# Scores of three batches on half-height PE tiles, and signs of six weight chunks made by ACT and POOL

## The chip, the cores and the metric

The kernel runs on one core of a Trainium2 chip. Time is device time in microseconds of one execution of the whole program. The core has a matrix engine (PE), which multiplies a stationary operand of up to 128 x 128 (loaded by PEld) with a moving one of up to 512 columns and writes PSUM; a vector engine (DVE); an activation engine (ACT); GpSimd (POOL), which cannot read PSUM; and a queue engine (SP), which here issues every DMA. Each engine works through its own instructions in program order, and waits on semaphores for the others.

## What is computed

Eight batches, eight heads, 512 positions (S), 32 states (NS) and head width 64 (D):

```python
scores = scale * x @ state.T;  a  = softmax(scores)   # over the 32 states
xread  = a @ state                                    # 512 x 64 a head
scores2 = scores.T;            a2 = softmax(scores2)  # over the 512 positions
sread  = a2 @ x                                       # 32 x 64 a head
y = concat([xread, sread], axis=positions)            # 544 rows of 512 channels
gate = sigmoid(causal_conv(y, conv_w, 5 taps))
out  = (gate * (y @ w_val)) @ w_out
```

x and state are float32. w_val, conv_w and w_out arrive as 64-bit floats (512 x 512, 5 x 512, 512 x 512); the kernel turns each into float32 by integer operations on its two 32-bit words.

## The kernel before

**Order by hand.** The program is a list of steps (`op(...)`), numbered as they are defined; ORDER lists these numbers in the order in which they are issued, and a letter behind a number names the engine where a step can run on several (a ACT, v DVE, g POOL). What an engine does next is thus fixed by ORDER alone. Tiles come from rings of a few buffers (`tiles`); a step that takes a buffer anew waits for the readers of what was in it.

**Weights.** For each of the four 128-row chunks of w_val and w_out, `words` issues five steps on 128 x 512 elements: `words_scale` (L205; the upper word read as a float, times 2^-112, into wc), `words_low` (L213; the lower word shifted right, into ws), `words_clamp` (L218), `words_join` (L223; wc shifted left, or ws) and `words_sign` (L228; sign bit of the upper word, or ws). The last runs on DVE and writes the weight: wv for w_val, ws in place for w_out. The words of a chunk lie in buffers shared with other tiles (vw0, ow0 with al; vw1, ow1 with swl), two of each; SP's load of a w_out chunk waits until the steps on the w_val chunk before it in that buffer are done. Each w_out chunk is then split in a high part `woh` (`high`, L234) and a low rest `wol` (`low`, L237), which the final projections use.

**Batches 0 to 2 (LONG)** load x in long runs of memory: partition p holds positions 4p to 4p+3. `x_T` (L303) transposes two positions (a pair, u = 0 or 1) of one head at a time, so that rows 0 to 63 of xT belong to u = 0 and rows 64 to 127 to u = 1. `long_scores` (L333) multiplies xT with the states over all 128 rows; `long_state` holds, for each u, the states in that half and zeros in the other, put there by `long_clear` (six memsets on POOL) and `long_T` (twelve scales). The output is written with stride so that the positions of a head come out in order. Batches 3 to 7 use `scores` (L311), with 64-row tiles, from the start.

**After the scores** a batch goes two ways. Over the states: `scores_T` (L387, 32 x 32 block transposes into sl), `max_n`, `sub_n`, `exp_n`, `sum_n`, `scale_n` and `probs` (L411, transpose back); then, but for batch 0, `high` and `low` split the probabilities into ah and al. Over the positions: `max_s` (L344), `exp_s` (L347, with a sum read out), `exp_T` (PE transposes), `state_read`. `read` (L416) makes xread in four PSUM tiles xr, which share the ring of the scores (sc, four buffers). `gate_first`, `gate_tap`, `gate_last`, `gate_add`, `gate` make the gate from xr. For batch 0 the convolution is done by PE (`read_conv`, L430) and `gate_read` (L451, ACT) makes the gate straight from PSUM. `values` (L475) multiplies the probabilities with state times w_val; `gated` (L486) joins both, `high` and `low` split g into gh and gl, and `project` (L496) multiplies with w_out: twelve matmuls per 128 positions, which need gh and gl of all four chunks of the batch. `project_copy` and `store` end it. The 32 state rows of all batches are done at the end (`tail`). `warm_up` (L240) is PE work without use, placed by ORDER.

Of the kernel before, what the change touches and what calls it, by code (L numbers as in the profile page):

```python
# [9 lines left out]
F32 = mybir.dt.float32  # L10
# [12 lines left out]
P = 128  # L23
# [46 lines left out]
def state_attention_gated_kernel(  # L70
# [45 lines left out]
        nb=(4, [P, NG], F32), sum2=(4, [P, NG], F32), r2=(2, [P, NG], F32),  # L116
# [5 lines left out]
        wc=("g", F32), ws=("o", I32), sTl=("last", F32), z5=("zc", F32), vw0=("al", I32), vw1=("swl", I32), ow0=("al", I32), ow1=("swl", I32),  # L122
# [23 lines left out]
    for name, shape, dt in (  # L146
        ("ident", [P, P], F32), ("wv", [P, NPR, C], F32), ("woh", [P, NPR, C], F32R), ("wol", [P, NPR, C], F32R),
        ("cw", [P, TAPS, NPR], F32), ("ones", [P, 2], F32),
        ("sel", [TAPS * NPR, TAPS, P], F32), ("cwb", [P, TAPS, P], F32),
        ("z", [P, B, NG, D], F32), ("xt", [P, NPR, B, HALO + NS], F32),  # L150
    ):
        fixed[name,] = const.tile(shape, dt, name=name)
    ident, wv, woh, wol, cw, ones, sel, cwb, z, xt = (
        fixed[n,] for n in ("ident", "wv", "woh", "wol", "cw", "ones", "sel", "cwb", "z", "xt"))
# [73 lines left out]
    def words_sign(word, dst, *key):  # L228
        hi = word()[..., 1]
        p, n = hi.shape  # L230
        nc.vector.scalar_tensor_tensor(
            dst().bitcast(I32), hi, SIGN, get("ws", *key)[:p, :n], op0=ALU.bitwise_and, op1=ALU.bitwise_or)

# [87 lines left out]
    def long_clear(b, u):  # L321
        nc.gpsimd.memset(long_state(b, u)[halves(u)[1]], 0.0)

    def long_state(b, u):
        return get("sTl", b)[:, u * H * NS:(u + 1) * H * NS].rearrange("p (k u n) -> p k u n", u=2, n=NS)

    def long_T(e, b, u, t):
        own, to = halves(u)[0], halves(t)[0]
        scale(
            e, long_state(b, t)[to, :, u], get("sgp", 0)[own].rearrange("p (k i n) -> p k i n", k=NPR, i=SB)[:, :, b],  # L330
            SCALE)

    def long_scores(b, g):  # L333
        for u in range(2):
            for q in range(SB):
                h = NG * q + g
                nc.tensor.matmul(
                    get("sc", b, g)[NS * q:NS * q + NS].rearrange("n (p v u) -> n u v p", v=2, u=2)[:, u],
                    long_state(b, u)[:, h // 2, h % 2],
                    get("xT", b, h // 2)[:, h % 2 * 256:h % 2 * 256 + 256].rearrange("d (v p) -> d v p", v=2),  # L340
                    start=True, stop=True, tile_position=(0, NS * q))
# [9 lines left out]

    def exp_T(b, g):
        for j in range(NJ):
            t = get("e2", b, g).rearrange("q (p j) -> q j p" if b in LONG else "q (j p) -> q j p", j=NJ)
            nc.tensor.transpose(get("e2p", b, g)[:, j * P:(j + 1) * P], t[:, j], ident)  # L355
# [14 lines left out]
    def sum_s(b):  # L370
        r2 = get("r2", b)
        nc.vector.tensor_scalar_add(r2, get("sum2", b), EPS)
        nc.vector.reciprocal(r2, r2)
# [195 lines left out]
    def words(src, fn, *key):  # L569
# [4 lines left out]
        op(words_sign, src, fn, *key)  # L574
# [7 lines left out]
    def group(r):  # L582
        op(group_T, r)
        op(state_T, r)
        for b in LONG if r == 0 else ():
            for u in range(2):
                op(long_clear, b, u)
                for t in range(2):
                    op(long_T, b, u, t)
    def batch(b):  # L590
# [10 lines left out]
        if b not in LONG:  # L601
            op(scores, b)
        for g in range(NG):
            if b in LONG:
                op(long_scores, b, g)
            op(scores_T, b, g)
            op(max_s, b, g)
            op(exp_s, b, g)
# [5 lines left out]
        op(probs, b)  # L614
# [120 lines left out]
```

## Time and profile before

| | us |
|---|---|
| three runs | 249.08, 247.27, 248.54 |
| median | 248.54 |
| the profiled execution: time | 247.3 |
| its span on the core | 245.5 |
| ORDER: steps on PE, DVE, ACT, POOL, SP | 188, 289, 268, 93, 85 |

A profile line names source line, engine, operation, and output<-inputs by the program's names. Busy times of the engines overlap; what sets the time is the chain of waits, and the stage in which an engine is full. A row of the stages has, behind the stretch and its length, busy time and count for each engine, the granted clock, the DMA share and GB/s. The trace shows a clock of 1.00 throughout. A matmul of 32-bit floats stands as two or more records.

### The profile page before, as it was taken

How to read it: one execution, taken by the hardware profiler on the slowest of the kernel's cores; microseconds unless marked ns; L12 is line 12 of the kernel's file. 1: busy time of each engine (PE TensorE's matmuls, PEld its weight loads, DVE VectorE, ACT ScalarE, POOL GpSimd, SP SyncE). 2: the span in 40 equal slices, each digit the busy share in tenths (PEclk: the TensorE clock that was granted, in tenths of full speed). 3: DMA queues.
4: the chain of work that ended last, by engine and by line, in shares of the span. 5: the costliest groups of instructions: out<-in, count | busy, mean ns of one | idle time of the engine just before them, and what ended most of it. 6: DMA issues, size and time to landing. Idle time of an engine off the chain costs nothing.

```text
span 245.5 us, 5051 instructions
## 1 busy us (share of the span) xinstructions
PE 231.2 (94%) x1955; PEld 167.7 (68%) x1955; DVE 206.3 (84%) x325; ACT 151.0 (62%) x321; POOL 127.0 (52%) x101
## 2 busy tenths in 40 slices
PE   7976999899999999999999999999999999978994
PEld 7953463366677884866787778666766768867882
DVE  3299999999898998899899898998997899987200
ACT  2056977788647875754787769785696475433110
POOL 3001146289959267793575689928758380131200
PEclk9999999999999999999999999999999999999999
DMA  6939987000320309213801021110110302300224
GB/s 194 312 105 341 340 190 169 7 3 0 88 78 10 85 24 277 62 28 88 225 34 53 3 96 62 69 43 3 43 44 3 132 0 85 128 0 3 85 76 138
DMA packets 34549, 22.88 MB, mean 93 GB/s; under 512 B 26058, under 2 KB 29150, under 8 KB 34526
## 3 DMA queue, kind: packets, MB, share of 16 engines
q1 hardware_dynamic: 34526, 22.57, 30.2%
q8 instruction: 15, 0.25, 0.4%
q14 instruction: 8, 0.07, 0.1%
HBM read 13.65 MB, written 8.91 MB: 92 GB/s over the span
## 4 chain that ended last, share of the span: by engine, by line
PE 62%; DVE 24%; DMA 5%; issue 4%; ACT 2%; SPq 1%; DVEq 0%; ACTq 0%
PE val L484 12%; PE op L492 11%; PE op L494 10%; PE op L493 10%; DMA vw<-w_val 4%; PE xTp L309 3%; DVE acc L461 3%; PE xr L421 3%; DVE tacc L518 3%; PE srp L365 3%; DVE g L487 2%; PE e2p L355 2%; PE sgv L287 2%; PE sc L315 2%; DMA ow<-w_out 2%
## 5 line engine op out<-in xcount | busy, mean ns | idle before, releaser
L461 DVE SCALAR_TENSOR_TENSOR acc<-xr,cw,acc 128x509 f32<-128x509 f32 (+2 forms) x84 | 60.6, 739 | 3.8 <-ACT xt L457 2.7
L492 PE MATMUL op<-woh,gh 128*128 128x512 f32 x128 | 52.1, 407 | 1.5 <-DVE g L487 1.1
L494 PE MATMUL op<-woh,gl 128*128 128x512 f32 x128 | 50.4, 394 | 0.0
L493 PE MATMUL op<-wol,gh 128*128 128x512 f32 x128 | 50.1, 392 | 0.0
L175 POOL TENSOR_TENSOR acc<-acc,last 128x508 f32<-128x508 f32 x22 | 28.6, 1304 | 27.6 <-DVE acc L461 22.5
L175 POOL TENSOR_TENSOR gl<-g,gh 128x512 fp32r<-128x512 f32 x25 | 33.0, 1326 | 9.0 <-ACT gh L162 8.4
L492 PEld LDWEIGHTS op<-woh,gh 128*128 128x128 f32 x128 | 24.0, 188 | 13.5 <-DVE g L487 4.0
L162 ACT COPY o<-op 128x512 f32<-128x512 f32 x26 | 15.3, 590 | 21.6 <-PE op L494 21.6
L175 POOL TENSOR_TENSOR ex<-ex,rc 128x1024 f32<-128x1024 f32 x8 | 15.4, 1919 | 25.3 <-DVE rc L406 23.5
L494 PEld LDWEIGHTS op<-woh,gl 128*128 128x128 f32 x128 | 24.0, 188 | 5.4
L493 PEld LDWEIGHTS op<-wol,gh 128*128 128x128 f32 x128 | 24.1, 188 | 4.6
L484 PE MATMUL val<-ah,swh 128*128 128x512 f32 x56 | 24.1, 430 | 1.1 <-DVE g L487 1.1
L473 ACT ACTIVATE sig<-acc 128x512 f32<-128x512 f32 x28 | 17.8, 637 | 9.1 <-POOL acc L175 6.2
L487 DVE SCALAR_TENSOR_TENSOR g<-sig,val 128x512 f32<-128x512 f32 x32 | 21.5, 674 | 2.2 <-PE val L484 1.0
L309 PE MATMUL xTp<-ident,x 128*128 128x128 f32 x128 | 19.2, 279 | 3.7 <-DMA x<-x 2.2
L162 ACT COPY xT<-xTp 128x512 f32<-128x512 f32 x29 | 17.1, 594 | 9.0 <-PE xTp L309 8.8
L484 PE MATMUL val<-ah,swl 128*128 128x512 f32 x56 | 22.1, 395 | 0.0
L484 PE MATMUL val<-al,swh 128*128 128x512 f32 x56 | 22.1, 394 | 0.0
L456 ACT ACTIVATE acc<-xr,cw 128x512 f32<-128x512 f32 x28 | 19.3, 699 | 4.3 <-PE xr L421 3.9
L162 ACT CAST gh<-g 128x512 fp32r<-128x512 f32 x24 | 15.1, 633 | 9.8 <-DVE g L487 9.8
L309 PEld LDWEIGHTS xTp<-ident,x 128*128 128x128 f32 x128 | 14.3, 140 | 9.9 <-issue 1.9
L175 POOL TENSOR_TENSOR al<-sl,ah 128x1024 fp32r<-128x1024 f32 x7 | 17.1, 2443 | 4.5 <-ACT xt L162 3.6
(132 smaller groups left out, 456.3 us busy)
## 6 DMA issues: line engine op xcount, KB each, us to landing
x<-x SPq DMA_DIRECT2D x32, 256.0 KB
out<-o SPq DMA_DIRECT2D x32, 256.0 KB
vw<-w_val SPq DMA_DIRECT2D x4, 512.0 KB
ow<-w_out SPq DMA_DIRECT2D x4, 512.0 KB
sg<-state SPq DMA_DIRECT2D x8, 64.0 KB
z<-state SPq DMA_DIRECT2D x16, 32.0 KB
out<-to SPq DMA_DIRECT2D x8, 64.0 KB
cww<-conv_w SPq DMA_DIRECT2D x1, 20.0 KB
```

Of the source, the lines that this page charges most:

```text
L162: nc.scalar.copy(out, in_)
L175: (nc.vector if e == "DVE" else nc.gpsimd).tensor_tensor(out, a, b, op=how)
L309: nc.tensor.transpose(get("xTp", b, pr)[:, j * P:(j + 1) * P], t, ident)
L365: nc.tensor.matmul(get("srp", b)[NS * q:NS * q + NS, g * D:(g + 1) * D], get("e2T", b, g)[:, j, NS * q:NS * q + NS], heads[:, j, NG * q + ...
L456: nc.scalar.mul(get("acc", b, pr), pt, cw[:, HALO, pr:pr + 1])
L461: nc.vector.scalar_tensor_tensor(acc[:, d:], get("xr", b, pr)[:, :S - d], cw[:, HALO - d, pr:pr + 1], acc[:, d:], op0=ALU.mult, op1=ALU.add)
L473: nc.scalar.activation(get("sig", b, pr), get("acc", b, pr), AF.Tanh, scale=0.5)
L484: nc.tensor.matmul(get("val", b, k), w, a, start=(i == 0), stop=(i == len(parts) - 1))
L487: nc.vector.scalar_tensor_tensor(get("g", b, k), get("sig", b, k), 1.0, get("val", b, k), op0=ALU.add, op1=ALU.mult)
L492: nc.tensor.matmul(pt, gh, woh[:, k], start=(k == 0), stop=False)
L493: nc.tensor.matmul(pt, gh, wol[:, k], start=False, stop=False)
L494: nc.tensor.matmul(pt, gl, woh[:, k], start=False, stop=(k == NPR - 1))
```

## The change

Two things are changed by hand, and ORDER is written anew for all steps.

**Scores of batches 0 to 2.** The states lie once in a fixed tile `both` (rows 0 to 63 and 64 to 127 hold the same), filled by four `long_T` of 64 x 384 instead of twelve of 64 x 128; the memsets are gone. `long_scores` works on tiles of 64 rows x 32 columns, and writes u = 0 and u = 1 to two PSUM tiles: sc(b, u) has half the positions of all heads, where sc(b, g) had all positions of half the heads. What follows is adapted: `long_max` and `long_max_both` for the maximum over both halves, four `long_exp` of 256 columns for two `exp_s` of 512, sums from two parts, and `long_probs`, which transposes 128 x 256 four times and writes every second element, for one transpose of 128 x 1024.

**Signs.** For chunks 1 and 3 of w_val and all four of w_out, `words_sign` is replaced by two steps: ACT takes the sign of the upper word (as -1, 0 or 1, into a buffer of `sig`), and POOL multiplies it into the joined words.

```diff
-        wc=("g", F32), ws=("o", I32), sTl=("last", F32), z5=("zc", F32), ...
+        sgn=("sig", F32), wc=("g", F32), ws=("o", I32), z5=("zc", F32), ...
+    def words_sgn(word, *key):
+        nc.scalar.activation(get("sgn", *key), word()[..., 1].bitcast(F32), AF.Sign)
+    def words_signed(word, dst, *key):
+        nc.gpsimd.tensor_tensor(dst().bitcast(F32), get("ws", *key).bitcast(F32), get("sgn", *key), op=ALU.mult)
...
-    def long_scores(b, g):
-        for u in range(2):
+    def long_scores(b):
+        for g in range(NG):
             for q in range(SB):
-                h = NG * q + g
-                nc.tensor.matmul(
-                    get("sc", b, g)[NS * q:NS * q + NS].rearrange("n (p v u) -> n u v p", v=2, u=2)[:, u],
-                    long_state(b, u)[:, h // 2, h % 2],
-                    get("xT", b, h // 2)[:, h % 2 * 256:h % 2 * 256 + 256].rearrange("d (v p) -> d v p", v=2),
-                    start=True, stop=True, tile_position=(0, NS * q))
+                for u in range(2):
+                    r = slice(D * u, D * u + D)
+                    c = slice(g * S // 2, (g + 1) * S // 2)
+                    nc.tensor.matmul(
+                        get("sc", b, u)[NS * q:NS * q + NS, c].rearrange("n (p v) -> n v p", v=2),
+                        both[r, q, g, b], get("xT", b, q)[r, c].rearrange("d (v p) -> d v p", v=2),
+                        start=True, stop=True, tile_position=(D * u, NS * q))
...
+    def long_max(b, u):
+        nc.vector.tensor_reduce(
+            get("nbl", b)[:, u], get("sc", b, u).rearrange("p (g t) -> p g t", g=NG), axis=AX.X, op=ALU.max,
+            negate=True)
+    def long_max_both(b):
+        nc.vector.tensor_tensor(get("nb", b), get("nbl", b)[:, 0], get("nbl", b)[:, 1], op=ALU.min)
+    def long_exp(b, g, u):
+        c = slice(g * S // 2, (g + 1) * S // 2)
+        nc.scalar.activation(
+            get("e2", b, g)[:, u * S // 2:(u + 1) * S // 2], get("sc", b, u)[:, c], AF.Exp,
+            bias=get("nb", b)[:, g:g + 1], accum_out=get("suml", b)[:, u, g:g + 1])
...
+    def long_probs(b, u):
+        a = get("sl" if b > 0 else "a0", b).rearrange("p g (t u) -> p u g t", u=2)[:, u]
+        ex = get("ex", b).rearrange("p (u g k) n -> p u g (k n)", u=2, g=NG)[:, u]
+        for g in range(NG):
+            nc.vector.transpose(a[:, g], ex[:, g])
...
-        op(words_sign, src, fn, *key)
+        if key in SIGNED:
+            op(words_sgn, src, *key)
+            op(words_signed, src, fn, *key)
+        else:
+            op(words_sign, src, fn, *key)
```

The new ORDER has 937 steps for 923. On the whole, by engine: PE 198 (warm_up 31 for 18), DVE 298 (low 17 for 10, high 11 for 7), ACT 270, POOL 86 (low 32 for 39, high 7 for 9, sub_n 7 for 5), SP 85. What stands ahead of the first `read` (batch 1), which both orders put after the work of batch 0, and on ACT ahead of the last `gate_read`, before -> after; a kind that isn't named has the same count:

| engine | steps ahead |
|---|---|
| DVE | words_sign 7 -> 2; words_scale 5 -> 2, that of conv_w 1 -> 0; words_clamp 5 -> 6; words_join 7, words_low 8 in both; max_s 6 -> 0, long_max 0 -> 6, long_max_both 0 -> 3; probs 2 -> 0, long_probs 0 -> 4 (of two transposes each); long_T 0 -> 2; sub_n 2 -> 1, scale_n 0 -> 1; copy of xT 1 -> 0; gated 1 -> 0; state_val_low 1 -> 2; read_last_copy 0 -> 1 |
| ACT | words_sgn 0 -> 5; words_scale 3 -> 5; exp_s 4 -> 0, long_exp 0 -> 12; long_T 12 -> 2; state_val_high 2 -> 4; high 13 -> 14; read_last_copy 0 -> 2 |
| POOL | words_signed 0 -> 5 |
| PE | warm_up 15 -> 29; exp_T 3 -> 5; values of batch 0 3 -> 2; read_last 2 -> 3; long_scores of three batches in both |

Behind that read, until the first `project`, DVE has in the new order: one words_join, four gated of batch 0 and one of batch 1, six gate_tap and one gate_add of batch 1, low of the probabilities of batch 1 and four more low, the last of which is gl of the last chunk of batch 0. PE has: that read, state_read of batch 1, the other two values of batch 0, one exp_T, three x_T, two values of batch 1, state_read_T, state_val of batch 3.

SP's order begins before with chunk 3 of w_val, conv_w, two heads of x of batch 0, chunks 1, 0 and 2, the states of batches 0 to 3, the rest of x of batch 0, and chunk 2 of w_out; after with chunks 2 and 3 of w_val, conv_w, chunk 0, two heads of x, the states, the rest of x of batch 0, chunk 1, six heads of x of batch 1, and chunk 3 of w_out.

More of the change, by code (lines that the diff above doesn't have):

```diff
@@ L121, in state_attention_gated_kernel @@
     alias = dict(
-        wc=("g", F32), ws=("o", I32), sTl=("last", F32), z5=("zc", F32), vw0=("al", I32), vw1=("swl", I32), ow0=("al", I32), ow1=("swl", I32),
+        sgn=("sig", F32), wc=("g", F32), ws=("o", I32), z5=("zc", F32), vw0=("al", I32), vw1=("swl", I32), ow0=("al", I32), ow1=("swl", I32),
         sg=("acc", F32), a0=("ah", F32), sw0=("swh", F32),
@@ L148, in state_attention_gated_kernel @@
         ("cw", [P, TAPS, NPR], F32), ("ones", [P, 2], F32),
-        ("sel", [TAPS * NPR, TAPS, P], F32), ("cwb", [P, TAPS, P], F32),
+        ("both", [P, NPR, 2, len(LONG), NS], F32), ("sel", [TAPS * NPR, TAPS, P], F32), ("cwb", [P, TAPS, P], F32),
         ("z", [P, B, NG, D], F32), ("xt", [P, NPR, B, HALO + NS], F32),
@@ L152, in state_attention_gated_kernel @@
         fixed[name,] = const.tile(shape, dt, name=name)
-    ident, wv, woh, wol, cw, ones, sel, cwb, z, xt = (
-        fixed[n,] for n in ("ident", "wv", "woh", "wol", "cw", "ones", "sel", "cwb", "z", "xt"))
+    ident, wv, woh, wol, cw, ones, both, sel, cwb, z, xt = (
+        fixed[n,] for n in ("ident", "wv", "woh", "wol", "cw", "ones", "both", "sel", "cwb", "z", "xt"))
     def two(t):
@@ L317, in scores, with long_T @@
                     start=True, stop=True, tile_position=(D * g, NS * q))
[L321 to L327, printed above, removed]
+    def long_T(e, u, t):
         own, to = halves(u)[0], halves(t)[0]
         scale(
-            e, long_state(b, t)[to, :, u], get("sgp", 0)[own].rearrange("p (k i n) -> p k i n", k=NPR, i=SB)[:, :, b],
+            e, both[to, :, u], get("sgp", 0)[own].rearrange("p (k i n) -> p k i n", k=NPR, i=SB)[:, :, :len(LONG)],
             SCALE)
-    def long_scores(b, g):
-        for u in range(2):
+    def long_scores(b):
+        for g in range(NG):
             for q in range(SB):
-                h = NG * q + g
-                nc.tensor.matmul(
-                    get("sc", b, g)[NS * q:NS * q + NS].rearrange("n (p v u) -> n u v p", v=2, u=2)[:, u],
-                    long_state(b, u)[:, h // 2, h % 2],
-                    get("xT", b, h // 2)[:, h % 2 * 256:h % 2 * 256 + 256].rearrange("d (v p) -> d v p", v=2),
-                    start=True, stop=True, tile_position=(0, NS * q))
+                for u in range(2):
[5 more added lines that the diff above has]
+                        start=True, stop=True, tile_position=(D * u, NS * q))
     def max_s(b, g):
@@ L350, in exp_s @@
             accum_out=get("sum2", b)[:, g:g + 1])
+    def long_max(b, u):
[9 more added lines that the diff above has]
+            bias=get("nb", b)[:, g:g + 1], accum_out=get("suml", b)[:, u, g:g + 1])
     def exp_T(b, g):
         for j in range(NJ):
-            t = get("e2", b, g).rearrange("q (p j) -> q j p" if b in LONG else "q (j p) -> q j p", j=NJ)
-            nc.tensor.transpose(get("e2p", b, g)[:, j * P:(j + 1) * P], t[:, j], ident)
+            if b in LONG:
+                t = get("e2", b, g)[:, j % 2 * S // 2:(j % 2 + 1) * S // 2].rearrange("q (p v) -> q v p", v=2)[:, j // 2]
+            else:
+                t = get("e2", b, g)[:, j * P:(j + 1) * P]
+            nc.tensor.transpose(get("e2p", b, g)[:, j * P:(j + 1) * P], t, ident)
     def exp_T_copy(e, b, g):
@@ L584, in group @@
         op(state_T, r)
[L585 to L589, printed above, removed]
+        for u in range(2 if r == 0 else 0):
+            for t in range(2):
+                op(long_T, u, t)
     def batch(b):
@@ L600, in batch @@
             op(high, lambda pr=pr: get("xT", b, pr), lambda pr=pr: get("xTp", b, pr))
-        if b not in LONG:
-            op(scores, b)
[L603 to L608, printed above, removed]
+        if b in LONG:
+            op(long_scores, b)
+            for u in range(2):
+                op(scores_T, b, u)
+                op(long_max, b, u)
+            op(long_max_both, b)
+            for g in range(NG):
+                for u in range(2):
+                    op(long_exp, b, g, u)
+        else:
+            op(scores, b)
+            for g in range(NG):
+                op(scores_T, b, g)
+                op(max_s, b, g)
+                op(exp_s, b, g)
         op(max_n, b)
@@ L613, in batch @@
         op(scale_n, b)
-        op(probs, b)
+        if b in LONG:
+            for u in range(2):
+                op(long_probs, b, u)
+        else:
+            op(probs, b)
         if b > 0:
```

78 lines of the change are left out of this document (42 added, 36 removed).

## The prediction

> **What bounds the kernel now.** I read the page first, then the stages, then the order of events where one limit hands over to another.
>
> ```profile
> span 245.5 us, 5051 instructions
> PE 231.2 (94%) x1955; PEld 167.7 (68%) x1955; DVE 206.3 (84%) x325; ACT 151.0 (62%) x321; POOL 127.0 (52%) x101
> PE 62%; DVE 24%; DMA 5%; issue 4%; ACT 2%; SPq 1%; DVEq 0%; ACTq 0%
> ```
>
> The chain that ended last is PE for 62% and DVE for 24%. The stages show which of them holds where (columns: stretch, its length, then busy time and count of PE, PEld, DVE, ACT, POOL, then clock and DMA):
>
> ```profile
> 12.00:20.00 8.00, 6.55 (x59) 4.00 (x59) 7.42 (x16) 4.42 (x12) 0.00 (x0) 1.00 0.49 158
> 20.00:30.00 10.00, 7.64 (x78) 4.50 (x79) 9.73 (x17) 8.37 (x19) 1.62 (x4) 1.00 1.03 343
> 30.00:40.00 10.00, 9.54 (x164) 5.66 (x163) 9.90 (x17) 8.49 (x18) 4.89 (x4) 1.00 0.79 182
> 40.00:50.00 10.00, 9.18 (x88) 3.92 (x87) 9.97 (x17) 7.00 (x17) 5.42 (x4) 1.00 0.26 60
> 50.00:95.00 45.00, 44.30 (x389) 31.50 (x388) 42.87 (x66) 32.87 (x71) 32.44 (x23) 1.00 0.21 57
> 95.00:195.00 100.00, 99.99 (x912) 72.29 (x911) 91.23 (x137) 71.51 (x153) 69.90 (x49) 1.00 0.23 70
> 195.00:227.00 32.00, 28.96 (x143) 23.71 (x142) 29.16 (x46) 14.36 (x30) 9.58 (x7) 1.00 0.11 41
> ```
>
> From 12 to 50 us DVE works 37.0 of 38 us and PE has gaps. From 50 on PE is full (44.3 of 45, then 99.99 of 100) and DVE has slack (8.8 us in 95 to 195). So the kernel has a DVE-bound front and a PE-bound rest, and the hand-over is the instruction where PE stops waiting for DVE. That is the read of batch 1:
>
> ```profile
> 47.89 1.47 PE L421 MATMUL xr<-sl,z 32*64 32x512 f32 x16 [0.82 <-DVE sl L412]
> 46.41 1.22 DVE L412 STREAM_TRANSPOSE sl<-ex 128x1024 f32<-128x1024 f32 x1
> 40.17 1.92 POOL L175 TENSOR_TENSOR ex<-ex,rc 128x1024 f32<-128x1024 f32 x1 [0.57 <-DVE rc L406]
> 40.22 2.41 DVE L231 SCALAR_TENSOR_TENSOR ws_o<-ow,ws_o 128x512 int32<-128x512 int32 x1
> 41.07 0.61 ACT L452 ACTIVATE sig<-xr 128x512 f32<-128x512 f32 x1
> ```
>
> PE's read of batch 1 starts at 47.89 and was released by DVE's transpose of that batch's probabilities (L412). Ahead of it, a sign step (L231) that began 0.05 us after a POOL product took 2.41 us, and ended 0.54 us after that product.
>
> So the sum is: how much earlier does read of batch 1 start, and does PE have more or less to do and to wait for behind it. The rows that price the steps (line, engine, shapes, count, busy and mean ns):
>
> ```profile
> L231 DVE SCALAR_TENSOR_TENSOR wv<-vw,ws_v 128x512 int32<-128x512 int32 x4 | 2.7, 683 | 0.0
> L231 DVE SCALAR_TENSOR_TENSOR ws_o<-ow,ws_o 128x512 int32<-128x512 int32 x4 | 5.5, 1375 | 0.0
> L172 DVE TENSOR_SCALAR wc_v<-vw 128x512 f32<-128x512 f32 x4 | 1.7, 424 | 8.6 <-DMA vw<-w_val 8.6
> L221 DVE TENSOR_SCALAR wc_v<-wc_v 128x512 f32<-128x512 f32 x4 | 1.6, 412 | 0.0
> L388 DVE STREAM_TRANSPOSE sl<-sc 128x512 f32<-128x512 f32 x16 | 10.8, 696 | 0.1
> L412 DVE STREAM_TRANSPOSE sl<-ex 128x1024 f32<-128x1024 f32 x7 | 8.6, 1226 | 0.0
> L373 DVE RECIPROCAL r<-r 128x2 f32<-128x2 f32 x8 | 1.3, 166 | 0.3
> L164 DVE COPY xT<-xTp 128x512 f32<-128x512 f32 x3 | 2.0, 660 | 0.0
> L170 ACT ACTIVATE sTl<-sgp 64x128 f32<-64x128 f32 x12 | 3.3, 272 | 12.6 <-PE sgp L276 11.8 <-PE sc L337 0.6
> L170 ACT ACTIVATE wc_o<-ow 128x512 f32<-128x512 f32 x3 | 2.1, 696 | 0.0
> L348 ACT ACTIVATE e<-sc,nb 128x512 f32<-128x512 f32 x16 | 11.0, 689 | 2.7 <-DVE nb L345 2.7
> L348 ACT ACTIVATION_READ_ACCUMULATOR e<-sc,nb 128x1 f32 x16 | 3.2, 202 | 0.0
> L400 ACT ACTIVATE ex<-sl 128x1024 f32<-128x1024 f32 x8 | 8.5, 1062 | 4.0 <-DVE sl L175 2.3 <-POOL sl L175 1.7
> L166 POOL TENSOR_TENSOR gh<-g,ones 128x512 fp32r<-128x512 f32 x6 | 6.3, 1042 | 2.4 <-DVE g L487 2.4
> L175 POOL TENSOR_TENSOR gl<-g,gh 128x512 fp32r<-128x512 f32 x25 | 33.0, 1326 | 9.0 <-ACT gh L162 8.4 <-PE sc L315 0.5
> L337 PE MATMUL sc<-xT,sTl 128*32 128x256 f32 x96 | 6.6, 384 | 0.1
> L315 PE MATMUL sc<-xT,sT 64*32 64x512 f32 x80 | 5.4, 601 | 0.0
> ```
>
> Back to back, an instruction costs some 0.08 us less than its length. In the chain of waits a sign step (0.683 long) stands so:
>
> ```profile
> 15.64 0.61 DVE wv L231
> ```
>
> So I use mean less 0.08 on DVE.
>
> **DVE ahead of the read of batch 1, by the two orders.** Counts are those of the table of the change; only differences count.
> - Signs: five words_sign fewer (7 to 2), 5 x 0.60 = -3.0. One of them was the held one: 2.41 - 0.68 = -1.73 more.
> - words_scale: three fewer on DVE, 3 x 0.34, and the small one of conv_w: -1.15. One clamp more: +0.34.
> - One xT copy fewer (to ACT): -0.6. One sub_n fewer, one scale_n of the same 128x1024 more: 0. One gated fewer, one state_val_low more, both 128x512: 0.
> - long_max has the form of max_s (128x512 in, two results for one): 0. long_max_both is new and tiny; the nearest row is the 128x2 reciprocal, 0.17, so 3 x 0.17 = +0.5.
> - long_T: two of four on DVE, 64x384 out of PSUM, not in the trace. Between 0.27 (ACT, 64x128) and 0.66 (DVE, 128x512); I take 0.5, nearer to the larger: +1.0.
> - long_probs: four 128x256 transposes for one of 128x1024. From 0.696 at 512 and 1.226 at 1024 columns, 0.43 at 256, so 4 x 0.35 = 1.4 against 1.15: +0.3 a batch, two batches, +0.6. Writing every second element shows nowhere; if it halved the rate, each would take 0.70 and a batch +1.3, the upper end; no reason for a gain.
> - One tiny copy: +0.15.
>
> Sum -3.9 us, between -5 and -2. The start I leave at zero: SP issues the same loads first (w_val, conv_w, the states of the first group, x of batch 0), in another order. Read of batch 1 then starts at about 44.0.
>
> **PE.** The three batches' scores fall from 96 matmul records of 128 rows to 96 of 64 rows, two row halves in two banks. The nearest row is L315, where two row halves also alternate, 5.4 us for 5 batches, 1.1 a batch; L337 cost 2.2 a batch. So 1.1 to 2.2 a batch, I take 1.1. The 3.3 us saved lie before 44 us, where PE has gaps, so they count nothing unless PE becomes late there. Likewise the 14 warm-ups more ahead of this read (29 for 15): they lie in PE's gaps (4.3 us of 12 to 40, and the time before the loads land). If that cover goes, they cost 0.45 each, 6.3 at most:
>
> ```profile
> 101.41 0.45 PE warm L243 x4
> 162.04 0.44 PE e2p L355 x4
> 43.37 3.70 PE L484 MATMUL val<-a,sw 128*128 128x512 f32 x8
> ```
>
> Behind the read, PE has one values of batch 0 more to do (3.70 for two: +1.85), two exp_T fewer (-0.88), one warm-up fewer (-0.45), one read_last fewer (-0.15): +0.4. The first project is then released by gl of the last chunk of batch 0. DVE has about 12.0 us ahead of that behind the probabilities (four gated and one of batch 1 at 0.6, six taps at 0.66, a gate_add at 0.9, four low at 0.6, one at 1.15, one join), PE about 11.5 in the same stretch. With the handing over, PE waits about 1.0 us there: +1.0.
>
> **POOL, ACT and SP.** POOL gets six products (1.04 to 1.33 each) and loses six memsets and seven low; it works 1.6 and 4.9 of 10 us in 20 to 40, so I cost them at nothing as POOL time. ACT gets five signs ahead of the read, like words_scale on ACT 0.70 each; its idle time hides them, see the second rival. SP's first w_out load waited for DVE's sign of a w_val chunk; now it waits for ACT's sign of chunk 3, early in ACT's order:
>
> ```profile
> SPq L199 <- DVE wv L231: 3.9, 1, 3.9
> ```
>
> Behind it x of batch 1 was queued, but DVE was busy all along (9.73 of 10 in 20 to 30), so an earlier x frees nothing: 0.
>
> **Sum.** -3.9 + 0.4 + 1.0 = -2.5 us. The profiled execution took 247.3; so 244.8 by it. The median of the three runs is 248.5, 1.2 above that execution; I take half of that: 245.4.
>
> **Rivals.**
> 1. The hold moves instead of going (about 248.6). The ws_o sign steps took 5.5 us for four where 2.7 is normal. Ahead of the read POOL now runs five products of signs, while seven joins stay on DVE with two SBUF inputs, as the sign had. If each product holds a DVE step for half its 1.3 us, 3.2 us come back, and the gain is gone. Against it, no join was held:
>
> ```profile
> L226 DVE SCALAR_TENSOR_TENSOR ws_o<-wc_o,ws_o x4: 670/678/683, 24.6 to 48.1; 128x512 int32<-128x512 int32 x4
> ```
>
> They are 0.683 at most, though POOL was busy a third of 20 to 40. The Trainium skill (SBUF — State Buffer, Who interferes with whom) says that a DVE instruction with two SBUF inputs contends with a GpSimd instruction that reads SBUF, and that the loser blocks for the whole instruction. The 2.41 us agree; by that rule the joins are as exposed as the signs were.
> 2. Slower: ACT becomes the front's limit (about 251.2). Ahead of the last gate_read of batch 0, ACT gets 5 signs (+3.5), 2 words_scale (+1.4), 12 half exponentials for 4 whole ones (a half is 0.689 less 256 columns at 0.373/512, so 0.50, plus 0.20 read-out: 8.4 - 3.6 = +4.8), 5 copies and scales (+2.1), 10 small scales fewer (-2.7): +9.1 us. Before, that gate_read ended at 41.68 (41.07 + 0.61), so 2.3 us remain to 44.0, and ACT's idle time from 12 to 40 is 6.7 us (28 less 4.42, 8.37, 8.49). 9.0 of cover for 9.1: just enough. If ACT fills none of the 6.7, the gate_reads end at 50.8, the read, which needs their PSUM, comes 2.9 later than before, and with the +0.4 the sum is 250.6 by the profiled execution, 251.2 by the same half step as above. There is no gain left once ACT fills less than some 3.3 us of its gaps.
> 3. Sign isn't in ACT's loaded table. One load ran, for exp and tanh together:
>
> ```profile
> L170 ACT ACT_TABLE_LOAD x1 | 1.3, 1283 | 0.7 <-PEq L724 0.7
> ```
>
> Then each sign between exponentials costs two loads, 2.6 us; with three such ahead of the read ACT is 7.7 us later and the time about 255. The Trainium skill (ScalarE: Activation LUTs, Table sets: the hidden batching unit) says that cheap functions stand in every set, naming relu, copy, identity and abs, not sign; it gives some 2.66 us for a switch. No run here shows it yet.
> 4. More than forecast (about 242): DVE also gets the scores of batch 0 earlier, 1.1 us for both halves instead of
>
> ```profile
> 17.28 2.67 PE L337 MATMUL sc<-xT,sTl 128*32 128x256 f32 x32
> ```
>
> and the second held sign, behind the read, goes too (5.5 - 2.7 - 1.73 = 1.1).
>
> **How the numbers follow.** Forecast 0.46, rival 1 0.18, rival 2 0.17, rival 3 0.03, rival 4 0.16. The predicted time is that of the forecast, 245.4. Range 241.8 to 251.2: from rival 4 to rival 2. A measurement of this kernel tells about 1%, 2.5 us, from no change. Faster by more than that is below 246.0: rival 4 and most of the forecast, 0.55. Within: the rest of it, rival 1 and part of rival 2, 0.29. Slower, above 251.0: part of rival 2, rival 3, 0.16.
>
> **What would show it.** Read of batch 1 (PE, xr<-sl,z, its first record) near 44 instead of 47.9, released by DVE. No words_sign held; joins at 0.68. Sign on ACT near 0.7 and a single table load. long_probs pieces near 0.43, long_scores near 1.1 a batch. PE full from about 55 on, DVE some 90% there. I am wrong if that read waits for ACT, if joins or low on DVE show 1.5 us and more beside POOL, if PE gets gaps in 95 to 195, or if DVE comes late for the last gated.

## The result: 2.7% slower, and the profile after

The changed kernel takes 254.59 us (median of 6 runs, 253.75 to 255.11) where the kernel before takes 248.58 in the same measurement: ratio 1.0274, 95% interval 1.0237 to 1.0311. The prediction, 245.4 us within 241.8 to 251.2, was wrong, in sign and in range. The profiled execution took 254.3 us.

Ahead of any row, the account that the rest goes by. TensorE (PE) ends the kernel, so the time is: when the read of batch 1 starts, plus PE's own work behind it, plus what PE waits behind it. For the waits I took every PE step behind that read and counted what it took beyond its shortest instance in the traces of before and after. All numbers in us:

| | read of batch 1 | PE waits behind it | last PE step ends |
|---|---|---|---|
| before | 47.89 | 18.0 | 241.88 |
| after | 47.42 | 25.2 | 248.80 |

The work left over is 176.0 in the one (241.88 - 47.89 - 18.0) and 176.2 in the other; counted by the shortest instances, it tells only that PE's list of steps behind the read weighs nearly the same. So the front gained 0.5 us where I forecast 3.9, and the part behind it lost 7.2 where I forecast 1.0.

The page of the changed kernel: span and size, busy time by engine, and the chain that ended last, which is followed back only a short way here:

```profile
span 252.4 us, 5171 instructions
PE 237.5 (94%) x2007; PEld 173.3 (69%) x2007; DVE 214.2 (85%) x340; ACT 154.2 (61%) x329; POOL 126.7 (50%) x94
PE 6%; DVE 2%; issue 1%; ACT 1%; ACTq 0%
```

DVE is busy for 7.9 us more than before (214.2 against 206.3), though signs were taken from it. The stages of the changed kernel, in the same columns as before:

```profile
12.00:20.00 8.00, 7.94 (x84) 6.44 (x83) 5.28 (x11) 4.08 (x9) 3.75 (x3) 1.00 0.73 261
20.00:30.00 10.00, 9.26 (x112) 6.65 (x100) 9.72 (x18) 9.21 (x23) 1.76 (x2) 1.00 0.78 267
30.00:40.00 10.00, 9.29 (x145) 4.91 (x145) 9.39 (x21) 9.31 (x31) 8.11 (x6) 1.00 0.69 157
40.00:50.00 10.00, 8.71 (x175) 4.92 (x170) 9.73 (x19) 7.53 (x16) 4.91 (x3) 1.00 0.01 2
50.00:95.00 45.00, 44.32 (x326) 29.75 (x325) 43.24 (x71) 32.42 (x68) 24.04 (x16) 1.00 0.38 96
95.00:195.00 100.00, 97.53 (x806) 70.78 (x805) 94.23 (x137) 69.72 (x146) 64.50 (x44) 1.00 0.18 57
195.00:227.00 32.00, 30.53 (x221) 24.23 (x220) 28.91 (x43) 17.30 (x37) 16.41 (x11) 1.00 0.17 63
```

Two rows stand out. In 12 to 20 DVE, the limit of the front, works 5.28 of 8 us where it worked 7.42: it waits there. In 95 to 195 PE has gaps where it had none (97.53 of 100 for 99.99), and DVE works 3.0 us more.

**The front.** In time order on PE, then on DVE (the second number is the length; in brackets the idle time before and what ended it):

```profile
12.51 2.82 PE L251 MATMUL warm<-ident 128*128 128x128 f32 x20
15.16 0.60 PE L284 MATMUL sgp<-ident,sg 128*128 128x128 f32 x4
...
47.42 1.21 PE L451 MATMUL xr<-sl,z 32*64 32x512 f32 x16 [0.59 <-DVE sl L439]
```

```profile
15.96 0.18 DVE L258 COPY cw<-cwp 128x20 f32<-128x20 f32 x1 [2.62 <-PE cwp L255]
...
43.68 2.29 DVE L177 TENSOR_TENSOR ex<-ex,rc 128x1024 f32<-128x1024 f32 x1
...
47.42 1.47 DVE L228 SCALAR_TENSOR_TENSOR ws_o<-wc_o,ws_o 128x512 int32<-128x512 int32 x1
...
148.32 2.40 DVE L429 TENSOR_SCALAR sm<-sm 128x32 f32<-128x32 f32 x1
...
158.28 4.11 DVE L177 TENSOR_TENSOR gl<-g,gh 128x512 fp32r<-128x512 f32 x2
```

Five warm-ups (21 to 25: 20 records, 2.82 us) stand in PE's order ahead of `group_T`, the transposes of the states. DVE has nothing to do until PE has made cwp behind them, and idles 2.62 us.

**The middle.** PE's waits there, and beside them what POOL does at the places where the DVE rows above are long:

```profile
151.71 0.50 PE L514 MATMUL val<-ah,swh 128*128 128x512 f32 x1 [0.61 <-DVE g L517]
...
155.71 0.53 PE L514 MATMUL val<-ah,swh 128*128 128x512 f32 x1 [0.54 <-DVE g L517]
...
162.44 0.51 PE L524 MATMUL op<-woh,gl 128*128 128x512 f32 x1 [0.55 <-DVE gl L177]
...
170.20 1.10 PE L451 MATMUL xr<-sl,z 32*64 32x512 f32 x10 [0.37 <-DVE acc L491]
```

```profile
148.27 2.42 POOL L177 TENSOR_TENSOR al<-sl,ah 128x1024 fp32r<-128x1024 f32 x1
...
158.19 1.32 POOL L177 TENSOR_TENSOR acc<-acc,last 128x508 f32<-128x508 f32 x1 [1.71 <-DVE acc L491]
159.46 2.37 POOL L177 TENSOR_TENSOR ex<-ex,rc 128x1024 f32<-128x1024 f32 x1
```

Each of these PE waits is for DVE. A small add of 128x32 takes 2.40 us, from 0.05 after the start of POOL's low half (al) to its end; the same form takes 0.18 at six other places of this kernel, and 0.92 at one, beside POOL again. Two low halves (gl) take 4.11 together, where one alone takes 0.65 to 0.69. In the count of the table above, PE waits 7.2 us in the steps that start between 148 and 177, 5.2 more than before in the same stretch; before, no step from 93 to 177 waited more than 0.24. The groups say why DVE is there at all (first row before, the others after):

```profile
L175 DVE TENSOR_TENSOR gl<-g,gh 128x512 fp32r<-128x512 f32 x7 | 5.7, 829 | 0.8 <-ACT gh L162 0.7
```

```profile
L177 POOL TENSOR_TENSOR gl<-g,gh 128x512 fp32r<-128x512 f32 x20 | 26.7, 1338 | 17.8 <-ACT gh L164 11.7 <-DVE gh L166 5.7
L177 DVE TENSOR_TENSOR gl<-g,gh 128x512 fp32r<-128x512 f32 x12 | 13.8, 1154 | 0.3
...
L240 POOL TENSOR_TENSOR ws_o<-ws_o,sgn_o 128x512 f32<-128x512 f32 x4 | 5.4, 1352 | 8.9 <-ACT sgn_o L237 7.6 <-DVE nb L361 1.4
...
L439 DVE STREAM_TRANSPOSE sl<-ex 128x256 f32<-128x256 f32 x8 | 2.9, 414 | 0.4 <-POOL ex L177 0.3
L237 ACT ACTIVATE sgn_o<-ow 128x512 f32<-128x512 f32 x4 | 2.8, 708 | 0.0
...
L164 ACT ACT_TABLE_LOAD x1 | 1.3, 1283 | 0.7 <-PEq L767 0.7
```

Five of the 25 low halves that POOL made went to DVE, 5.7 -> 13.8 us: that is as much as DVE's whole increase. At 0.68 us each, the five are an estimated 3.4 us; the other 4.7 are time that low halves spend held beside POOL (their mean goes from 829 to 1154 ns).

**The tail.** ACT's copy of project(7,2) stands behind a gate that waits 4.27 us for DVE, and PE's next project waits for the buffer which that copy frees:

```profile
232.63 0.63 ACT L553 ACTIVATE tsig<-tacc 128x512 f32<-128x512 f32 x1 [4.27 <-DVE tacc L548]
233.17 0.57 ACT L164 COPY o<-op 128x512 f32<-128x512 f32 x1
```

```profile
233.79 0.51 PE L522 MATMUL op<-woh,gh 128*128 128x512 f32 x1 [1.57 <-ACT o L164]
```

### The profile page after: what moved, and what is told of

The parts are those of the page before. It is cut to its first block, busy times and chain, and to the rows that moved or that the text cites. A ratio compares the mean times of both kernels' runs of the same rounds, so it can differ in the third digit from the quotient of the medians.

```text
span 252.4 us, 5171 instructions
## 1 busy us (share of the span) xinstructions
PE 237.5 (94%) x2007; PEld 173.3 (69%) x2007; DVE 214.2 (85%) x340; ACT 154.2 (61%) x329; POOL 126.7 (50%) x94
## 5 line engine op out<-in xcount | busy, mean ns | idle before, releaser
L491 DVE SCALAR_TENSOR_TENSOR acc<-xr,cw,acc 128x510 f32<-128x510 f32 (+2 forms) x84 | 60.0, 739 | 1.6 <-ACT xt L487 0.5
L177 POOL TENSOR_TENSOR acc<-acc,last 128x508 f32<-128x508 f32 x22 | 29.2, 1330 | 23.4 <-DVE acc L491 18.4
L177 POOL TENSOR_TENSOR gl<-g,gh 128x512 fp32r<-128x512 f32 x20 | 26.7, 1338 | 17.8 <-ACT gh L164 11.7
L164 ACT COPY o<-op 128x512 f32<-128x512 f32 x29 | 17.1, 589 | 29.9 <-PE op L524 29.8
L164 ACT COPY xT<-xTp 128x512 f32<-128x512 f32 x31 | 18.3, 607 | 16.7 <-PE xTp L317 16.7
L177 POOL TENSOR_TENSOR ex<-ex,rc 128x1024 f32<-128x1024 f32 x7 | 14.1, 2018 | 21.2 <-ACT o L164 6.4
L503 ACT ACTIVATE sig<-acc 128x512 f32<-128x512 f32 x28 | 17.7, 634 | 10.0 <-POOL acc L177 8.2
L317 PE MATMUL xTp<-ident,x 128*128 128x128 f32 x128 | 18.9, 277 | 1.1 <-ACT xT L164 0.7
L251 PE MATMUL warm<-ident 128*128 128x128 f32 x124 | 17.5, 299 | 1.4 <-POOL ident masks.py:199 1.4
L251 PEld LDWEIGHTS warm<-ident 128*128 128x128 f32 x124 | 16.3, 212 | 1.9 <-POOL ident masks.py:199 1.4
```

The lines of the kernel that those rows point to most:

```text
L164: nc.scalar.copy(out, in_)
L177: (nc.vector if e == "DVE" else nc.gpsimd).tensor_tensor(out, a, b, op=how)
L251: nc.tensor.matmul(get("warm", i)[:, j * P:(j + 1) * P], ident, ident, start=True, stop=True)
L317: nc.tensor.transpose(get("xTp", b, pr)[:, j * P:(j + 1) * P], t, ident)
L491: nc.vector.scalar_tensor_tensor(acc[:, d:], get("xr", b, pr)[:, :S - d], cw[:, HALO - d, pr:pr + 1], acc[:, d:], op0=ALU.mult, op1=ALU.add)
L503: nc.scalar.activation(get("sig", b, pr), get("acc", b, pr), AF.Tanh, scale=0.5)
```

## The experiments

**Theory A**: neither edit of the code costs the time; the newly written order does, at three places: warm-ups ahead of `group_T`, DVE in the middle, the copy in the tail. **Rival B**: the edits themselves collide. **Rival C**: the middle has too much DVE work in any order. **Rival D**: what is saved at one place waits at the next. ORDER's numbers are written below as the steps they stand for, with the letter of the engine behind them; `low<gated(4,1)` is the low half of what gated(4,1) made. Lines left out are marked `...`. Ratios are to the kernel before on the same chip.

**e1: signs alone, e2: scores alone, on the order of before.**

```diff
+words_sgn(o,0)
 words_join(o,0)
...
-words_sign(o,0)
+words_signed(o,0)
```

> The old order and the old scores; only the signs of the six chunks are made by ACT (words_sgn where words_join stood, just ahead of it) and multiplied in by POOL (words_signed where words_sign stood). Theory A, the loss of 6 us is in the new order and not in the signs: DVE loses six sign steps and both held ones (3.6 + 2.7 us), the read of batch 1 starts 2 to 4 us earlier than 47.9, and the time is 244 to 248. Theory B, the signs themselves cost it (POOL's products hold DVE's two-input steps, ACT is late): joins or low steps on DVE show 1.5 us and more, the read comes at 48 or later, time 250 or more.

```diff
-long_scores(1,1)
-max_s(1,1)
+long_scores(1)
+long_max(1,1)
+long_max(1,0)
+long_max_both(1)
...
-long_scores(1,0)
...
-max_s(1,0)
```

> The old order with the new scores and the old signs; where two steps became one, it stands at the place of the first, and the maxima of batches 1 and 2 stand together. Theory A, the loss is in the new order: DVE has some 1.5 us more to do ahead of the read of batch 1 (the tiny maxima, the split transposes), ACT some 3 us more, PE 3 us less where it has gaps; the time is 247.5 to 250.5. Theory B, the halved scores cost it: 252 or more, with ACT or DVE late ahead of the read of batch 1.

e1: 246.60 us, ratio 0.9969 (0.9930 to 1.0008); read at 46.12, 1.8 earlier than before and short of the 2 to 4 expected; waits behind 17.7. e2: 248.64 us, 1.0013 (0.9970 to 1.0057); read at 49.71, waits 18.3. Neither edit slows the kernel on the old order, and the waits behind the read stay those of before. In e1 two joins, of 0.68 otherwise, are held beside POOL's sign products. DVE, then POOL:

```profile
16.27 1.64 DVE L227 SCALAR_TENSOR_TENSOR ws_v<-wc_v,ws_v 128x512 int32<-128x512 int32 x1
...
35.65 1.64 DVE L227 SCALAR_TENSOR_TENSOR ws_o<-wc_o,ws_o 128x512 int32<-128x512 int32 x1
```

```profile
16.07 1.30 POOL L239 TENSOR_TENSOR wv<-ws_v,sgn_v 128x512 f32<-128x512 f32 x1 [7.92 <-ACT xT L163]
...
35.42 1.31 POOL L239 TENSOR_TENSOR ws_o<-ws_o,sgn_o 128x512 f32<-128x512 f32 x1 [3.20 <-DVE ws_o L227]
```

**e5: both edits, on the order of before** (the two diffs together).

> Both edits of the code, on the order of before: each long-run step stands where its forerunner stood, each Sign just ahead of its join, each POOL product where the DVE sign stood. Theory A (the loss is in the rewritten order, not in the two edits): the two single edits measured 0.9969 and 1.0013 of before, so both together 246 to 249 us, the waits of TensorE behind the first tap read near 18 us as before, the read of batch 1 between 46 and 49 us. Rival B (the two edits collide with each other, on POOL or on the port that DVE and POOL share, and the order has little to do with it): 252 to 255 us, with the waits behind the read near 25.

248.74 us, ratio 1.0080 (1.0035 to 1.0124), read at 48.37, waits 19.2. Within theory A's numbers, and far from rival B's: of the 2.7% some 0.8 come with the two edits, the rest with the order. The read is no earlier than before, and the granted clock (third column from the end) drops in the front of the profiled executions of e5 and of e2, which it doesn't in those of before, after or e1. First e2, then e5:

```profile
12.00:16.00 4.00, 1.74 (x8) 1.13 (x8) 3.12 (x8) 0.61 (x2) 0.00 (x0) 0.81 0.36 116
16.00:20.00 4.00, 3.75 (x22) 2.32 (x26) 3.96 (x9) 2.71 (x6) 0.00 (x0) 0.50 0.54 182
```

```profile
16.00:20.00 4.00, 1.90 (x35) 0.50 (x33) 3.93 (x8) 2.69 (x6) 1.32 (x1) 1.00 0.80 249
20.00:25.00 5.00, 3.92 (x18) 2.92 (x19) 4.96 (x9) 3.46 (x9) 1.13 (x2) 0.66 1.04 330
```

**e4: the changed kernel without warm-ups 21 to 25.**

```diff
 conv_spread(0)
-warm_up(21)
-warm_up(22)
-warm_up(23)
-warm_up(24)
-warm_up(25)
 group_T(0)
```

> The changed kernel without five warm-ups, which stand on PE between conv_spread and the transposes of the states (12.5 to 15.3 us). Theory A, they hold the front up: the transposes of the states start about 2.5 us earlier, DVE's idle 2.6 us ahead of conv_copy goes, the read of batch 1 starts 1.5 to 2.5 earlier than 47.4, and the time falls by 1 to 2.5 us. Theory B, the states' DMA has not landed earlier, or a wait behind takes the place: the transposes start at 14.5 or later, time within 0.6 of 254.6.

251.99 us, ratio 1.0172 (1.0102 to 1.0241); span 249.8, 2.6 less; waits behind the read unchanged at 25.2. The read comes 2.6 earlier:

```profile
44.82 1.21 PE L451 MATMUL xr<-sl,z 32*64 32x512 f32 x16 [0.60 <-DVE sl L439]
```

**e3: the tail's copy ahead of the gate.**

```diff
+project_copy(7,2) a
 tail_gate(1)
 tail_gated(1)
 store(6,0)
-project_copy(7,2) a
```

> The changed kernel, with one step moved: ACT's copy of the output of project(7,2) stands ahead of tail_gate(1) instead of behind it. Theory A, the end loses time because that copy waits in ACT's order behind a gate that waits for DVE's taps, while PE waits for the PSUM buffer: the wait of 1.6 us ahead of project(7,1) goes, and the one of 0.7 later may stay; time 1.5 to 2.5 below the changed kernel's 254.6. Theory B, the end is set by DVE's taps and tail_gated anyway: less than 0.6 below it.

253.10 us, ratio 1.0200 (1.0117 to 1.0282), which overlaps the changed kernel's, though its executions (252.08 to 253.12) all lie below that kernel's (253.75 to 255.11); the wait ahead of PE's next project is gone (1.73 us by steps) and the waits behind the read fall from 25.2 to 23.3.

**e6: the middle.**

```diff
-low<probs(5) g
...
 low<gated(4,2) g
+low<probs(5) g
...
+low<gated(4,1) g
...
-low<gated(4,1) v
-low<gated(4,3) v
+low<gated(4,3) g
```

> The changed kernel with three steps of batches 4 and 5 moved, nothing else: the low halves of gated(4,1) and gated(4,3) from DVE to POOL, and the low half of probs(5) on POOL behind that of gated(4,2) instead of beside DVE's small add of sum_n(6). Theory A (TensorE's waits between 148 and 171 us come from DVE instructions held beside POOL ones: 2.40 for 0.18, 1.78 and 2.40 for 0.68, and 1.1 elsewhere): the three held ones go, DVE gains some 5 us there, TensorE's excess behind the read falls from 25.2 to between 20 and 23, and the time from 254.6 to 250 to 253. Rival C (the order simply puts too much work of DVE ahead of what TensorE needs there; holds are only where DVE's lateness shows): the waits stay within 1.5 us of 25.2 and the time within 1.5 us of 254.6.

251.62 us, ratio 1.0196 (1.0143 to 1.0250); waits 22.5. The small add takes 0.18 again. But two waits stay in the middle, 1.97 and 0.79: POOL makes al too late, and a DVE cast is held in turn. PE, then DVE:

```profile
156.65 0.50 PE L514 MATMUL val<-al,swh 128*128 128x512 f32 x1 [1.59 <-POOL al L177]
```

```profile
154.55 2.33 DVE L166 CAST gh<-g 128x512 fp32r<-128x512 f32 x1
```

**e7: e3, e4 and e6 together.**

> The changed kernel with three places of its order mended together: without warm-ups 21 to 25, with the copy of project(7,2) ahead of the last tail gate on ACT, and with the three moves of e6. Theory A (three separate losses, each in its own stretch): 2.6 from the warm-ups, 1.5 from the tail, 2 to 4 from the middle add up: 246.5 to 249.5 us, within 1% of before. Rival D (the losses cover each other: work saved in one place waits in the next): 250 to 252.5 us.

248.10 us, ratio 1.0037 (1.0004 to 1.0070); read at 45.84, waits 20.7. Taken singly the three are worth 1.02, 0.74 and 0.78% (1.0274 less 1.0172, 1.0200, 1.0196), 2.5 in all (each known to some 0.5 to 0.8); together 2.4. By the medians it is 2.6, 1.5 and 3.0 us, 7.1 in all, and 6.5 together. Within that noise they add up, so rival D falls for these.

**e8: the middle mended otherwise; e12: one step of it moved.**

First e8, against e7:

```diff
+low<probs(5) g
 low<gated(4,0) g
...
-low<probs(5) g
...
-high<gated(4,1) v
...
-high<gated(4,3) v
-low<gated(4,1) g
+high<gated(4,1) a
 gate(5,1)
...
+high<gated(4,3) a
 low<gated(4,3) g
+low<gated(4,1) g
```

> The kernel of e7 with the middle mended otherwise: the low half of probs(5) goes ahead of that of gated(4,0) on POOL instead of behind that of gated(4,2), and the high halves of gated(4,1) and gated(4,3) go from DVE to ACT, because e7 still shows 1.98 us of waiting at values(5,1), with two DVE casts held for 2.35 and 1.49 beside POOL. Theory A (holds are what TensorE waits for in the middle): the wait at values(5,1) goes, the excess behind the read falls from 20.7 to about 18.7, and the time from 248.1 to 246 to 246.8. Rival C (DVE's work is simply too much there): 247.6 to 248.6, with another wait of about 2 us between 150 and 172.

247.76 us, ratio 1.0016 (0.9989 to 1.0043); waits 20.1. The holds are gone (the add takes 0.28, the casts are on ACT), yet project(4,2) waits 1.81, which is what rival C expected. On DVE, POOL and PE:

```profile
157.45 0.69 DVE L517 SCALAR_TENSOR_TENSOR g<-sig,val 128x512 f32<-128x512 f32 x1 [2.58 <-POOL gl L177]
```

```profile
156.13 2.52 POOL L177 TENSOR_TENSOR gl<-g,gh 128x512 fp32r<-128x512 f32 x2 [2.03 <-ACT gh L164]
```

```profile
158.70 0.50 PE L524 MATMUL op<-woh,gl 128*128 128x512 f32 x1 [1.41 <-POOL gl L177]
```

DVE is idle here, not full: it waits for a buffer of g, which POOL frees late because gl of chunk 3, queued first, waits for a high half that ACT makes last. In e12 gl of chunk 1 goes first:

```diff
 high<gated(4,1) a
+low<gated(4,1) g
 gate(5,1)
...
 low<gated(4,3) g
-low<gated(4,1) g
```

> The kernel of e8 with one step moved: on POOL the low half of gated(4,1) goes ahead of that of gated(4,3). In e8 both stand behind the high half of gated(4,3), which ACT makes last; POOL is idle 2.03 us ahead of them, DVE 2.58 us for the buffer of g that they free, and TensorE 1.41 us for the second of them. Theory A: the wait at project(4,2) goes, excess behind the read 18.3 to 18.9, against 20.1 in e8 and 18.0 before; time 246 to 246.8. Rival C (DVE's work is too much there in any order): a wait of 1.5 us or more between 150 and 172 stays, time as e8 within 0.6 us.

246.26 us, ratio 0.9947 (0.9918 to 0.9975), half a per cent below the kernel before. Most of that goes with the granted clock: averaged over an execution it is 1.000 in all twelve of e12, but 0.986 to 0.999 in eleven of the seventeen of the kernel before in this measurement, and the six at 1.000 have a median of 246.44 us. So e12 wins the whole loss back; that its order is better at the same clock isn't shown. The largest wait left in the middle is 0.81, waits behind the read 18.9, and PE is full again:

```profile
95.00:195.00 100.00, 99.85 (x826) 73.82 (x825) 90.62 (x140) 71.56 (x150) 67.79 (x47) 1.00 0.19 61
```

For this last wait rival C falls: from e8 to e12 no step of DVE is added or taken. For the waits before it, place and amount aren't told apart: e6 and e8 also took two low and two high halves off DVE (busy 94.23 of 100 us in 95 to 195 in the changed kernel, 90.62 in e12, 91.23 before).

**e11: e7 without warm-ups 26 to 30 as well** (ten fewer in all).

> The kernel of e7 without warm-ups 26 to 30 as well. Question: do the further warm-ups do anything. e2 and e5 (the new score tiles on the old order) show the granted clock at 0.50 to 0.87 in stretches between 12 and 35 us where the tables of the new order show 1.00. Theory W (the added warm-ups keep the clock up): the clock falls below 0.9 in at least one stretch between 15 and 35 us, and the read of batch 1 comes 0.5 us or more later against the start of group_T than in e7 (32.65). Rival F (they are filler): clock 1.00 throughout, the read no later, time within 0.7 us of e7's 248.1.

247.88 us, ratio 1.0012 (0.9990 to 1.0035), as e7 within their intervals, and clock 1.00 in all stretches from 8 to 50 us, one of them

```profile
20.00:25.00 5.00, 3.51 (x31) 1.85 (x32) 4.96 (x9) 4.85 (x15) 1.27 (x1) 1.00 0.99 307
```

so the ten are filler in this order: theory W falls for them. Over all ten executions the mean clock is 0.997 or more.

**e9 and e10: the new front spliced to the old rest**, at the read and 20 steps later. Besides a few steps whose buffers weren't free, the copy of exp_T(2,1) follows the read at once in e9, and warm-ups 0 and 4 are left out of both.

> The order of e4 (the new one without warm-ups 21 to 25) up to the read of batch 1, and behind it the order of e5 (before's), with only the steps moved whose buffers are not yet free. Theory A (the new order is better ahead of the read by some 2 to 3 us and worse behind it by 7): read at 45 to 46.5, excess behind it 18 to 20, time 244.5 to 247, below before. Rival D (the earlier read is given back behind it, because DVE is not earlier with what follows): excess 20.5 or more, 247 to 249.

> As e9, with the seam 20 steps later, behind values(0,0): the first taps of batch 1 and the gated values of batch 0 still come in the new order. Theory A: within 1.5 us of e9, 244.5 to 247.5. Rival D: as for e9, 247 to 249.

e9: 247.99 us, ratio 1.0021 (0.9997 to 1.0044), read at 45.14, waits 21.8. e10: 251.64 us, 1.0178 (1.0137 to 1.0218), waits 24.6, of which 4.3 at a single step, state_val(3). Both miss theory A's numbers; e9 fits rival D's, and e10 lies above those too. e9's read comes 3.2 us earlier than e5's, but the first project starts at 65.52 and 65.51: what lies between was laid out for the later read, and DVE now idles twice for PE's values:

```profile
48.51 0.69 DVE L517 SCALAR_TENSOR_TENSOR g<-sig,val 128x512 f32<-128x512 f32 x1 [2.13 <-PE val L514]
...
51.34 0.69 DVE L517 SCALAR_TENSOR_TENSOR g<-sig,val 128x512 f32<-128x512 f32 x1 [2.15 <-PE val L514]
```

## Why the prediction was wrong, step by step

- **What bounds the kernel**: right. PE ends it, DVE bounds the front, and the read of batch 1 is the hand-over in both kernels.
- **DVE ahead of that read, -3.9**: the mechanism was right, the size 1.4 too large. DVE's records ahead of the read, each counted up to the start of the next, sum to 38.64 us before and 36.13 after, -2.5. The signs gave -4.7 as forecast (6.04 -> 1.37, the held one among them), long_T +0.94 for +1.0, the pieces of long_probs +0.4 for +0.6. Wrong was "one sub_n fewer, one scale_n more: 0": the scale_n takes 2.21 for 1.13, because it runs beside a POOL sign product (43.68, 2.29 long).
- **Warm-ups "lie in PE's gaps", nothing**: the first step that failed. Five of the 14 stand ahead of `group_T`, and DVE's idle time ahead of the read grows from 5.15 to 7.39 us. Taking them out gives back 2.6 us (e4); a PE gap ahead of a step that PE must do first isn't cover. For the other five that were tried (e11) it held.
- **Behind the read, +0.4 of work and +1.0 of waiting**: the second step that failed, and the larger. The work was right (176.0 and 176.2). The waits are +7.2: 5.2 of it between 148 and 177, some 2 from 195 on, and none up to and with the first project, where I had put the +1.0 (3.0 us there, 3.5 before). I listed what DVE does up to the first project and took the rest as it was, although the table of the change had seven more low and four more high steps on DVE in all, and I gave no term to what those cost. Those that PE came to wait for stand 100 us and more behind the read, beside POOL products. I also took DVE's slack of 8.8 us in 95 to 195 as cover, but slack over 100 us doesn't help where three held instructions fall within 14.
- **POOL, ACT and SP, 0**: right in the front but for the scale_n that POOL's product held; in the tail ACT's order cost 1.7 us of PE's time.
- **Rival 1, the hold moves**: its mechanism came true, at another place. In e1 two joins are held for 1.64; after the change one is (1.47, behind the read), and the costly ones are low halves and a small add in the middle. "No join was held" was a fact of the old order's timing and no evidence for the new one; and in the same old trace a low half on DVE was held (1.58 us at 200.16, to 0.54 after the end of a POOL add), which I overlooked. The rule of the Trainium skill that I set beside it (SBUF — State Buffer, Who interferes with whom) agrees: joins of 0.68 become 1.64.
- **Rival 2, ACT as the limit**: fell. The read waits for DVE (L439), and ACT's gaps filled (9.31 of 10 in 30 to 40).
- **Rival 3, another table**: fell. One load of 1283 ns with Exp, Tanh and Sign; a sign takes 0.708. The Trainium skill (ScalarE: Activation LUTs, Table sets: the hidden batching unit) doesn't list sign among the functions of a set; these runs show it beside exp without a second load.
- **Rival 4, more than forecast**: fell. With the warm-ups out the read comes at 44.82, near the 44.0 forecast but with an earlier start: counted from `group_T` it is 2.0 us sooner than before (32.7 for 34.7).
- **"I am wrong if ... low on DVE show 1.5 us and more beside POOL, if PE gets gaps in 95 to 195"**: both happened, so the signs to look for were named; what was missing was their price in the sum.

Still open are why e5 is 0.8% slower than before while e1 is not, since the clock drops there at the same time, and how the lowered clock comes about. Nine of e5's ten executions have a mean clock of 0.970 to 0.993, but the one at 1.000 took 248.37 us, so the clock alone doesn't settle it.

## What to carry to other kernels

When a change rewrites the order of all steps, count each engine's steps over the whole program before pricing the part that the change is about: here the two edits cost some 0.8% (0.35 to 1.24) and the order the rest of the 2.7%. A step of filler in an in-order queue is free only if nothing behind it is awaited. And an instruction's slack is local: look for what stands beside it on the engine that held it (here POOL for DVE), and for which buffer its reader frees.

## What the runs showed of the hardware

Which DVE instructions POOL holds is sharply divided. In the trace of the changed kernel, 41 taps that read PSUM (acc<-xr,cw,acc) run beside POOL at 0.71 to 0.75 us, as the others do (0.65 to 0.75), and reductions (max_n: 1.20 to 1.22 beside POOL, 1.21 without) and 32x32 transposes (128x512: 0.67 to 0.72 beside, 0.70 without) don't change either. The gl low halves, with two inputs in SBUF, take 0.65 to 0.69 in six places, where no POOL instruction runs, one is just ending, or they began first, and 1.17 to 2.40 in the other six, a 128x32 add 0.18 and up to 2.40, and a cast in e6 2.33: even the smallest waits for the end of the POOL instruction that it meets. The six held low halves each end 0.55 us after a POOL instruction, the add 0.04 after. This agrees with the Trainium skill (SBUF — State Buffer, Who interferes with whom), which states it of two SBUF inputs, says that casts and tensor_scalar can contend, and exempts reductions; the price of one meeting, up to 2.2 us for an instruction of 0.18, is these runs'.

The granted clock fell to 0.50 and 0.66 in stretches of the front of e2 and e5. Ahead of these stands a stretch in which PE was busy under half of the time (1.74 and 1.90 of 4 us). But both kernels drop to 0.66 once more in 30 to 35, behind stretches with 3.74 and 3.46 of 5, and before, with 2.65 of 5 in 20 to 25, keeps 1.00. Over whole executions, the kernels with the complete new order (after, e3, e4, e6, e7, e8, e11, e12; 62 executions) never show a mean clock below 0.997, while 10 of the 29 executions of the kernel before that were measured beside e8 lie at 0.986, with a median of 248.2 us against 246.9 for the 14 at 0.997 and more. So the new order goes with a steady clock, and the ten warm-ups that e11 leaves out aren't what does it. What decides it was not tried.
